# Reordering an attention-plus-S4 kernel, transposing x by DMA, keeping the last inverse matrix resident, and summing the complex product in TensorE

## The chip, the cores and the metric

The kernel runs on one core of one Trainium2 chip. The metric is the device time of one execution, in microseconds (us). One execution of each kernel was also recorded by the hardware profiler; all lines shown below come from such records. The engines are named PE (TensorE, matmuls), PEld (TensorE weight loads), DVE (VectorE), ACT (ScalarE), POOL (GpSimd) and SP (the engine whose queue issues most DMAs). An execution counts as fast unless it is over 1.5% above the fastest of the same kernel; comparisons use fast runs.

Before the change the kernel took 512.9 us (median of three runs, 511.55 to 514.36).

## The reference, cut to what matters

The output is two independent results side by side, both bf16, of 2048 positions by 640 channels.

```python
# part A: 32 heads of 20 channels, each position attends to itself and 7 earlier ones, 2 apart
qkv = x @ wqkv
attn = softmax(where(mask, einsum("bhsd,bhswd->bhsw", q, kg) * Dh**-0.5, -1e9))
o = einsum("bhsw,bhswd->bhsd", attn, vg);  a = o @ wo
# part B: S4 convolution, 640 channels, 192 states each
P = exp(dt * (A_re + 1j*A_im) * l)              # l = 0..2047: the powers
K = einsum("dn,dnl,dn->dl", C, P, dt*B).real    # the convolution kernel
y = irfft(rfft(u, 4096) * rfft(K, 4096))[:2048] + u * Dskip
```

## The kernel before: what the change touches

Part B works in five chunks of 128 channels. For each chunk VectorE builds two tables of powers, X and Y, by complex products of a few base powers; TensorE multiplies them into the convolution kernel `Kd` ("M" below, for make). `Kd` is spread into time order, the FFTs of u and K run as two matmul steps `f1` and `f2`, VectorE multiplies the two spectra, and a first inverse step `ia` gives Z ("F"). A second inverse step turns Z into y for chunks 0 to 2 together and later for 3 and 4 ("I"); y gets u times Dskip ("S"). Part A runs in four blocks: logits and softmax ("L"), weighted values and output projection ("V"). A scheduler interleaves all this at build time; after that every engine runs its instructions in a fixed order.

The base powers of a chunk pair come from ScalarE sines between two VectorE steps, and go through DRAM (`Gd`):

```python
for k in order:                                   # 11 powers of two
    pht = gp.tile(..., name="ph", tag="ph")       # one buffer each
    mct = gp.tile(..., name="mc", tag="mc")
    nc.scalar.activation(out=mc, in_=wi[:, s], func=ACT.Identity, bias=...)
    V.tensor_scalar(out=ph[:, 0], in0=mc, ..., op0=A.logical_shift_left)
    V.tensor_scalar(out=ph[:, 1], in0=wi[:, s], ..., op0=A.logical_shift_left)
    nc.scalar.activation(out=cs..., in_=ph..., func=ACT.Sin, scale=PHS)
    V.tensor_tensor(out=cs, in0=cs, in1=am..., op=A.mult)
    done(k, cs)                                   # DMA of cs to Gd
```

The spectrum product and the first inverse step:

```python
V.tensor_tensor(out=Y,    in0=K, in1=Ur..., op=A.mult)
V.tensor_tensor(out=t[:], in0=K, in1=Ui..., op=A.mult)
V.tensor_tensor(out=Y[:, :, 0], in0=Y[:, :, 0], in1=t[:, :, 1], op=A.subtract)
V.tensor_tensor(out=Y[:, :, 1], in0=Y[:, :, 1], in1=t[:, :, 0], op=A.add)
# ia: 16 j, 2 parts, 4 channel groups: 128 matmuls that each fill a quarter of the output rows
MM(ps[32*g:32*g+32, jj], lhsT=Yf[:, :, r, 4*j+g], rhs=C["EA"][:, r, :], ..., tile_position=(0, 32*g))
```

x comes in eight loads and is transposed by 80 matmuls with the identity, evicted by 24 ScalarE copies. The order of the main program:

```python
gens(..., 0, 1, dst0, done0)       # powers of chunk 0
make(0); a.transpose()
for ct in range(5): a.proj("k", ct)
for ct in range(5): a.proj("q", ct)
batch(1, 3); batch(3, 5)           # powers of chunks 1, 2 and of 3, 4
# ... u is reordered through DRAM ...
for ct in range(5): a.proj("v", ct)
make(1)
for c in range(NCH):
    # F(c), then make(c + 2), then (c < 4) L(c) V(c); for c == 3 the first inverse
inverse([3, 4], ...)
```

The second inverse step loads a quarter of its matrix `HB` at a time (two buffers), in both inverses, so the whole 4 MB comes twice. Each quarter then loads u, multiplies by HB, copies to `ysb` on ScalarE, makes `ud = u * D + ysb` on VectorE (one buffer), and stores.

The softmax here doesn't subtract the row's maximum and nothing guards it: scores larger than these inputs give would overflow.

## Time and profile before

| | before |
|---|---|
| time, median of 3 | 512.9 us |
| profiled execution, span and mean granted clock | 511.0 us, 0.876 |
| first attention product starts | 149.6 us |
| last power table ends | 369.7 us |
| HBM read | 42.86 MB |

The page's busy table, VectorE's row of the 40 slices (each digit the busy tenths of one fortieth of the span), and the chain of work that ended last, in shares of the span:

```profile
PE 368.9 (72%) x5943; PEld 243.2 (48%) x5943; DVE 360.2 (70%) x528; ACT 269.0 (53%) x517; POOL 104.8 (21%) x192
...
DVE  0326899651899997999999977998948753636012
...
PE 36%; DVE 28%; DMA 15%; ACT 12%; issue 6%; SPq 1%; POOL 0%; ACTq 0%; POOLq 0%; DVEq 0%
```

No engine is full over the whole span. VectorE is nearly full in the middle and has gaps at the beginning and the end. Cutting the span at the first attention product and at the end of the last table (within 0.9 us of them) shows the three stages. Columns of the windows view: stretch, its length, busy us (and instructions) of each engine, granted clock, DMA share, GB/s.

```profile
0.00:149.66 149.66, 109.90 (x1015) 56.24 (x1016) 90.10 (x188) 103.12 (x197) 47.88 (x83) 0.94 0.69 186
149.66:368.90 219.24, 166.70 (x3363) 121.96 (x3363) 205.68 (x273) 108.10 (x206) 26.19 (x57) 0.87 0.39 104
368.90:511.00 142.10, 92.25 (x1565) 65.02 (x1564) 64.38 (x71) 57.74 (x115) 30.72 (x52) 0.81 0.51 144
```

The middle stage is VectorE's: 205.68 of 219.24 us. In the first stage the waits view shows VectorE waiting for sines (engine, tile and line waited for, us in total, times, longest):

```profile
DVE cs L212 <- ACT cs L211: 22.3, 10, 9.7
```

In the last stage, loads and stores of the second inverse step stand in the way:

```profile
DVE ud L671 <- DMA out_dram<-ud: 18.3, 4, 8.3
...
PE ps_ib L667 <- DMA zq<-Zdram_61: 8.6, 2, 5.1
...
PE ps_ib L667 <- DMA HB<-k_HB: 8.3, 2, 5.6
```

And two groups that the change replaces, from the page (line, engine, operation, names, shapes and count, then busy us and mean ns of one, then idle before; for the DMA: count, size, us to landing):

```profile
L364 PE MATMUL ps_ia<-cEA,Yf 128*32 128x256 bf16 x640 | 29.1, 333 | 7.9 <-DVE Yf L350 6.7
...
HB<-k_HB SPq DMA_DIRECT2D x8, 1024.0 KB, 6.1
```

### The profile page before, as it was taken

What the parts mean: (1) busy time and instruction counts of PE and PEld (TensorE: products, weight loads), DVE (VectorE), ACT (ScalarE), POOL (GpSimd) and SP (SyncE); (2) the same over time, 40 slices, a digit from 0 to 9 for tenths busy, and PEclk for the clock granted to TensorE, in tenths of its full rate; (3) what the DMA queues carried; (4) which work ended last, traced back from release to release, by engine and by line L of the source; (5) the groups of instructions that cost most, each with busy time, mean ns of one, the idle gap of its engine ahead of it and who ended that gap; (6) DMA issues with size and microseconds to landing.
All of it is one profiled execution on the core that took longest, in us unless ns stands there. A gap on an engine that the chain in (4) does not pass through costs nothing.

```text
span 511.0 us, 13799 instructions
## 1 busy us (share of the span) xinstructions
PE 368.9 (72%) x5943; PEld 243.2 (48%) x5943; DVE 360.2 (70%) x528; ACT 269.0 (53%) x517; POOL 104.8 (21%) x192
## 2 busy tenths in 40 slices
PE   2868799874752778798879868699495855987720
PEld 1543334631220566666656755476263533765520
DVE  0326899651899997999999977998948753636012
ACT  4466895758682435656355723467224522656610
POOL 7605500055000001000170001070001341143012
PEclk9999999997795788799988978999779969997955
DMA  7964946359669352220236432043609597622262
GB/s 197 267 145 129 225 123 208 104 168 255 215 211 314 118 110 66 60 115 3 61 66 204 114 66 57 1 132 83 139 13 347 146 299 192 197 48 39 91 187 41
DMA packets 83596, 70.99 MB, mean 139 GB/s; under 512 B 51744, under 2 KB 75104, under 8 KB 81872
## 3 DMA queue, kind: packets, MB, share of 16 engines
q1 hardware_dynamic: 75456, 55.90, 39.0%
q0 software_dynamic: 6368, 13.16, 10.7%
q10 hardware_dynamic: 1712, 1.07, 0.8%
q8 instruction: 46, 0.75, 0.7%
q14 instruction: 14, 0.11, 0.1%
HBM read 42.86 MB, written 24.13 MB: 131 GB/s over the span
## 4 chain that ended last, share of the span: by engine, by line
PE 36%; DVE 28%; DMA 15%; ACT 12%; issue 6%; SPq 1%; POOL 0%; ACTq 0%; POOLq 0%; DVEq 0%
PE ps_o L493 6%; DVE krtmp L226 4%; PE ps_k L286 4%; PE ps_k L281 4%; PE ps_op L508 3%; DMA Gdram<-cs 3%; DMA xn<-in_A_x_dram 3%; PE ps_s L310 3%; ACT S L344 3%; DMA zq<-Zdram_61 3%; DMA out_dram<-ud 3%; DVE Ytab L225 3%; DVE prod L468 2%; PE ps_p L428 2%; DMA uq<-Udram 2%
## 5 line engine op out<-in xcount | busy, mean ns | idle before, releaser
L468 DVE TENSOR_TENSOR prod<-qb,kb 128x2048 bf16<-128x2048 bf16 x40 | 48.7, 1233 | 2.0 <-PE ps_l L471 2.0
L502 POOL DMA_DIRECT2D oT<-vb x64 | 36.7, 581 | 48.1 <-ACT vb L494 43.8
L429 ACT CAST st<-ps_p 128x512 bf16<-128x512 f32 x60 | 34.1, 581 | 12.6 <-PE ps_p L428 12.3
L428 PE MATMUL ps_p<-xT,w_324 128*128 128x512 bf16 x100 | 28.0, 439 | 13.7 <-ACT st L429 13.6
L364 PE MATMUL ps_ia<-cEA,Yf 128*32 128x256 bf16 x640 | 29.1, 333 | 7.9 <-DVE Yf L350 6.7
L494 ACT CAST vb<-ps_o 128x512 bf16<-128x512 f32 x20 | 13.1, 653 | 37.2 <-PE ps_o L493 37.1
L286 PE MATMUL ps_k<-Ytab,Xtab 64*20 64x33 bf16 x1280 | 25.8, 243 | 9.3 <-issue 9.2
L342 PEld LDWEIGHTS <-cT 128*64 128x64 bf16 x640 | 23.3, 114 | 18.9 <-issue 18.3
L288 ACT CAST Kd<-ps_k 128x363 bf16<-128x363 f32 (+1 forms) x15 | 6.8, 453 | 47.2 <-PE ps_k L286 47.2
L471 PE MATMUL ps_l<-prod,cGs 128*32 128x512 bf16 x160 | 18.3, 435 | 17.6 <-DVE prod L468 17.4
L225 DVE TENSOR_TENSOR Ytab<-Ytab 128x2688 bf16<-128x2688 bf16 (+3 forms) x25 | 30.8, 1234 | 0.0
L364 PEld LDWEIGHTS <-Yf 128*32 128x32 bf16 x640 | 23.3, 174 | 15.3 <-DVE Yf L350 8.2
L226 DVE TENSOR_TENSOR krtmp<-Ytab 128x2688 bf16<-128x2688 bf16 (+3 forms) x25 | 30.4, 1215 | 0.0
L281 PEld LDWEIGHTS <-Xtab 128*20 128x20 bf16 x1280 | 21.9, 125 | 14.9 <-issue 14.2
L493 PEld LDWEIGHTS <-cident 128*128 128x128 bf16 x160 | 14.9, 100 | 28.8 <-issue 14.4
L428 PE MATMUL ps_p<-xT,w_320 128*128 128x512 bf16 x100 | 25.6, 410 | 3.9 <-ACT st L429 2.8
L212 DVE TENSOR_TENSOR cs<-cs,am 128x768 bf16<-128x768 bf16 x22 | 12.2, 556 | 22.3 <-ACT cs L211 22.3
L292 POOL DMA_DIRECT2D Kd<-Kd x20 | 10.1, 514 | 86.6 <-ACT Kd L288 86.2
L286 PEld LDWEIGHTS <-Xtab 64*20 64x20 bf16 x1280 | 21.9, 121 | 12.2 <-issue 10.6
L244 POOL MEMSET Ytab<- 128x192 bf16 x5 | 1.4, 284 | 123.9 <-PE ps_k L286 123.9
L225 DVE TENSOR_TENSOR Xtab<-Xtab,Xg 128x768 bf16<-128x768 bf16 (+2 forms) x35 | 24.7, 706 | 2.2 <-DMA Xg<-Gdram 1.8
L281 PE MATMUL ps_k<-Ytab,Xtab 128*20 128x33 bf16 x1280 | 25.1, 246 | 1.1 <-DVE Ytab L229 0.5
(460 smaller groups left out, 948.7 us busy)
## 6 DMA issues: line engine op xcount, KB each, us to landing
HB<-k_HB SPq DMA_DIRECT2D x8, 1024.0 KB, 6.1
Gdram<-cs SPq DMA_DIRECT2D x24, 192.0 KB, 3.1
kb<-kd SPq DMA_DIRECT2D x4, 710.0 KB, 6.7
vb<-vd SPq DMA_DIRECT2D x4, 710.0 KB, 5.4
xn<-in_A_x_dram SPq DMA_DIRECT2D x8, 320.0 KB, 6.0
us<-in_B_u_dram POOLq DMA_DIRECT2D x16, 160.0 KB, 5.0
Udram<-uc POOLq DMA_DIRECT2D x8, 320.0 KB, 4.0
kd<-st SPq DMA_DIRECT2D x5, 512.0 KB, 5.8
```

Of the source, the lines that this page charges most:

```text
L225: V.tensor_tensor(out=full(O), in0=full(Y), in1=gb(gr), op=A.mult)
L226: V.tensor_tensor(out=full(t), in0=full(Y), in1=gb(gi), op=A.mult)
L281: MM(o, lhsT=X[:, :, part, col], rhs=Y[:, :, part, col], start=False, stop=False, tile_position=(0, 32 * g), skip_group_check=True)
L286: MM(o, lhsT=X[hb:hb + 64, :, part - 2, col], rhs=Y[hb:hb + 64, :, part - 2, col], start=False, stop=(part == 3), tile_position=(hb, 32 * ...
L342: nc.tensor.matmul(ps[64 * dd:64 * dd + 64, kk, r], lhsT=T[:, k, r, :], rhs=A1[:, k, :, 64 * dd:64 * dd + 64], start=(kk == 0 and r == 0), ...
L364: MM(o, lhsT=Yf[:, :, r, 4 * j + g], rhs=C["EA"][:, r, :], start=(jj == 0 and r == 0), stop=(r == 1), skip_group_check=True, tile_position ...
L428: nc.tensor.matmul(ps[:], lhsT=w[:, kt, 128 * ct:128 * ct + 128], rhs=self.xT[:, kt, 512 * sc:512 * sc + 512], start=(kt == 0), stop=(kt = ...
L429: nc.scalar.copy(out=st[:, sc], in_=ps[:])
L468: V.tensor_tensor(out=pr[:], in0=q[:, ct].unsqueeze(1).to_broadcast([128, 4, 4, 128]), in1=windows(k[:, ct, :, 8 - 8 * m:8 - 8 * m + 128], ...
L471: nc.tensor.matmul(ps[32 * sc:32 * sc + 32], lhsT=self.pools["Gs"][:, ct, :], rhs=pr[:, :, sc, :], start=(ct == 0), stop=(ct == 4), tile_p ...
L493: nc.tensor.matmul(ps[:], lhsT=self.ident[:], rhs=p2[:, w], start=(w == 0), stop=(w == W - 1))
L502: nc.gpsimd.dma_start(out=oT[32 * q:32 * q + 32, :, sc, :], in_=self.vb[qb][32 * sc:32 * sc + 32, q:DH:4, HALO:HALO + 128])
```

## The change

The intent has seven parts that are named or easy to see: (1) all base powers are made before the first table; (2) attention blocks move ahead and overlap other work, in an order given by a string; (3) x is transposed by DMA; (4) Z lives in two slots outside the tables' space, so that (5) the inverse matrix can be loaded once and stay; (6) VectorE makes only the four products of the complex multiplication, and TensorE sums them as four accumulated terms with full-width matmuls; (7) u times D is made ahead in four buffers, and the last inverse adds its matmul result to it straight from PSUM.

There are smaller parts that the description does not name: the loads of A, B and C of part B change queues, the phase tiles get a second buffer, the X table gets a new layout and one more product step, 15 zero matmuls go, and the shift of `Kd` moves 7 rows on two queues in place of 12 on one.

The core of the diff (cuts are marked):

```diff
+ORDER = "L0 V0 M1 F0 L1 V1 M2 F1 L2 V2 M3 F2 M4 F3 S012 I012 L3 F4 V3 S34 I34"
# ... constants: EA gets four slots; HB's rows are permuted; X_EXP reordered ...
-        eng[g % 2].dma_start(out=ldt[32 * g:32 * g + 32, :], in_=lsrc[g])
+        nc.scalar.dma_start(out=ldt[32 * g:32 * g + 32, :], in_=lsrc[g])
-            (eng[g % 2] if a < 2 else nc.gpsimd).dma_start(out=nat[a]...)   # eng = [sync, scalar]
+            (nc.gpsimd if a in (2, 3) else nc.sync).dma_start(out=nat[a]...)
# ... powers
-        pht = gp.tile([128, 2, 2 * CW], i32, name="ph", tag="ph")
-        mct = gp.tile([128, 2 * CW], i32, name="mc", tag="mc")
+        pht = gp.tile([128, 2, 2 * CW], i32, name="ph", tag="ph", bufs=2)
+        mct = gp.tile([128, 2 * CW], i32, name="mc", tag="mc", bufs=2)
# ... tables: new layout and steps; kgen: no zero matmul; Kd shift on two queues ...
# ... spectrum product
-        V.tensor_tensor(out=Y, in0=K, in1=Ur..., op=A.mult)
-        V.tensor_tensor(out=t[:], in0=K, in1=Ui..., op=A.mult)
-        V.tensor_tensor(out=Y[:, :, 0], in0=Y[:, :, 0], in1=t[:, :, 1], op=A.subtract)
-        V.tensor_tensor(out=Y[:, :, 1], in0=Y[:, :, 1], in1=t[:, :, 0], op=A.add)
+        for i, u in enumerate((Ur, Ui)):
+            V.tensor_tensor(out=Yf[:, 2 * i:2 * i + 2, :, 32 * b:32 * b + 32], in0=K, in1=u..., op=A.mult)
# ... ia
-            for r in range(2):
-                for g in range(4):
-                    MM(o, lhsT=Yf[:, :, r, 4 * j + g], rhs=C["EA"][:, r, :], ..., tile_position=(0, 32 * g))
+            for q in range(4):
+                nc.tensor.matmul(ps[:, jj]..., lhsT=Yf[:, q, 2 * jq + jj, :], rhs=C["EA"][:, q, :], start=(jj == 0 and q == 0), stop=(q == 3))
# ... x
-        for q in range(8):
-            xn = xw.tile([128, 2, D], bf16, name="xn", tag="xn", bufs=3)
-            nc.sync.dma_start(out=xn[:], in_=xsrc[:, 2 * q:2 * q + 2, :])
+        for q in range(4):
+            nc.sync.dma_start(out=self.xT[:, :, 512 * q:512 * q + 512], in_=self.x[0, 512 * q:512 * q + 512, :], transpose=True)
# ... 80 transposing matmuls and 24 copies go ...
     gens(tc, pools, ta, wi, 0, 1, dst0, done0)
+    batch(1, 3)
+    batch(3, 5)
     make(0)
-    a.transpose()
# ... after the k and q projections
-    batch(1, 3)
-    batch(3, 5)
# ... second inverse step
-            HB = ip.tile([128, 16, 2, 128], bf16, name="HB", tag="HB", bufs=2)
-            nc.sync.dma_start(out=HB[:]..., in_=hsrc[:, s])
+        inv["HB"] = HB = ip.tile([128, 64, 2, 128], bf16, name="HB")   # once, in two DMAs
+    Z = fp.tile([128, 2, 64, 2, 32], bf16, name="Z")
# ... skip(cs): ud = u * D ahead of its inverse, ud with bufs=4 ...
+                if n == 3:
+                    nc.scalar.copy(out=ysb[:, o:o + per], in_=ps[:])
+                else:
+                    V.tensor_tensor(out=ud[:, o:o + per], in0=ps[:], in1=ud[:, o:o + per], op=A.add)
```

In the letters of the order string, the program before ran M1 F0 M2 L0 V0 F1 M3 L1 V1 F2 M4 L2 V2 F3 L3 V3 I012 F4 I34.

## The prediction

> **What bounds the kernel now.** No engine is full: over 511 us TensorE is busy 72%, VectorE 70%, ScalarE 53% (busy table). By windows there are three stages. (1) 0 to 149.7 us, up to the first attention product: VectorE busy 90 us, ScalarE 103, TensorE 110; VectorE waits 22 us in all for sines (waits view). (2) 149.7 to 368.9, up to the end of the last power table: VectorE 206 of 219 us, so VectorE-bound. (3) 368.9 to 511, 142 us: TensorE 92, VectorE 64, ScalarE 58. The chain of waits shows loads of skip input (8.4 us), Z (9.6, 4.8), inverse matrix (5.6, 2.7), stores (7.2, 3.8), and the last chunk's FFT running alone.
>
> **What the change does, with durations from the trace.**
> - VectorE: the 40 add/subtracts of the complex product go (17.2 us). X tables get one more step, about +0.7 us per chunk. 360 becomes about 346 us.
> - ScalarE: 24 transposed-x copies (12.0 us) and 8 of the last inverse (4.7) go: 269 to about 252.
> - TensorE: 80 transposes (11 us) and 15 zero matmuls (5.9) go. The inverse-A step has 64 full 128x256 matmuls per chunk instead of 128 quarter ones: 36 ns each (56 in 2.01 us) becomes about 105 (the 128x256 spread matmuls run at 100), so +2 us per chunk. Net 369 to about 360.
> - DMA: the inverse matrix is loaded once, not twice (4 MB less), ahead of its use. x comes by four DMA transposes; no trace shows one. The Trainium skill (DMA: Bandwidth & Descriptors, "Latency and other measured facts") states 261 GB/s; my estimate from it is 10 us for 2.6 MB.
> - Order: all powers come before the first table; chunk 1's table now precedes the first product; attention block 3 overlaps the first inverse; only chunk 4's FFT and the short inverse follow.
>
> **On the critical path.** Summing durations along VectorE's new order: about 132 us precede the first product (89 before), about 167 lie between it and the last table (207 before), 44 follow. ScalarE has about 108 us up to the end of the powers and phase tiles are double-buffered, so VectorE starves less: the first product stays near 152 us with 43 us more VectorE work done. The middle shrinks to about 190 us (TensorE also has about 187 there), so the last table ends near 342 instead of 369. Tail: table-to-kernel matmuls 10, rest of chunk 3's FFT 20, first inverse with attention products 21, chunk 4's FFT 32 (ScalarE-bound: 44 evictions of about 0.65 us), output projection and last inverse 17, stores 5 to 8: about 107 instead of 142, because most waits for Z, matrix and skip input go.
>
> **Predicted: 455 us**, 8 in 10 between 432 and 482. Faster by over 2%: 0.93; within 2%: 0.05; slower: 0.02.
>
> **What would show it.** First product at 145 to 165 us; VectorE over 85% busy before it. Last table at 330 to 355. From there about 107 us to the end, with under 8 us of TensorE waiting for matrix or Z. VectorE busy about 346, TensorE 360, ScalarE 252. Inverse-A matmuls about 105 ns apart. DMA transposes landing before 30 us.
>
> **What would make it wrong.** DMA transposes much slower than 261 GB/s: ScalarE's fixed order has projection copies between sines, so a late x stalls the powers and everything after (+10 to +25 us). The powers' trip through DRAM delaying chunk 1's table. The inverse matrix reuses the table's space, so its load starts only after the last table matmuls; landing late, it holds the first inverse. [...]

## The result, and the profile after

The changed kernel took 466.03 us (median of four runs, 464.76 to 469.33) against 512.23 us for the kernel before (four runs). The ratio is 0.911, with a 95% interval of 0.904 to 0.918. Every ratio in this document is the mean time of one kernel's fast runs over that of the kernel before in the same rounds, so it is not quite the ratio of the medians quoted. The output was correct.

| | before | predicted | after |
|---|---|---|---|
| time | 512.2 us | 455 (432 to 482) | 466.0 us |
| first attention product starts | 149.6 | 152 (145 to 165) | 146.1 |
| last power table ends | 369.7 | 342 (330 to 355) | 354.7 |
| from there to the end | 141 | 107 | 108 |
| busy TensorE / VectorE / ScalarE | 369 / 360 / 269 | 360 / 346 / 252 | 367 / 347 / 254 |
| HBM read | 42.86 MB | | 36.18 MB |

The row of HBM reads overstates what was saved. Of what went, 4.19 MB are the second load of the inverse matrix (with it back, u_hb below reads 40.37 MB), but 2.62 MB are x itself: with the plain loads back, u_xpose reads 38.80 MB although its DMAs move the same 66.7 MB in all. So in these runs the count leaves out what the DMA transposes read. (The longer `EA` adds 0.13 MB.)

The page of the changed kernel, as shown of before:

```profile
PE 367.2 (79%) x5528; PEld 241.2 (52%) x5528; DVE 347.0 (75%) x513; ACT 254.0 (55%) x485; POOL 97.1 (21%) x173
...
DVE  1599797999599974899979899999998074740413
...
PE 38%; DVE 35%; DMA 9%; ACT 8%; issue 7%; POOL 1%; SPq 1%; POOLq 0%; DVEq 0%; ACTq 0%
...
L351 PE MATMUL ps_ia<-cEA,Yf 128*128 128x256 bf16 x320 | 37.7, 276 | 3.6 <-DVE Yf L341 3.6
...
HB<-k_HB SPq DMA_DIRECT2D x2, 2048.0 KB, 7.9
```

DMA has fallen from 15% to 9% of the chain that ended last and ScalarE from 12% to 8%; the two engines that do the arithmetic now hold 73% of it. The first inverse step costs TensorE 8.6 us more over five chunks (37.7 against 29.1). The windows, cut at the same two events:

```profile
0.00:146.20 146.20, 95.98 (x894) 45.05 (x895) 116.59 (x238) 91.06 (x168) 44.38 (x72) 0.84 0.74 193
146.20:354.30 208.10, 188.13 (x3184) 132.67 (x3185) 189.60 (x232) 108.55 (x209) 32.24 (x67) 0.93 0.45 117
354.30:463.00 108.70, 83.08 (x1467) 63.47 (x1457) 40.81 (x46) 54.44 (x109) 20.51 (x34) 0.89 0.47 130
```

In the middle stage TensorE and VectorE are now both near 90% busy. VectorE did 26.5 us more before the first product (116.59 against 90.10), not the 43 us of the prediction.

The waits view of the first stage, and TensorE's longest waits of the last stage:

```profile
PE ps_p L400 <- ACT st L401: 30.8, 6, 14.2
...
ACT cs L214 <- DMA Gdram<-cs: 12.5, 9, 3.1
...
DVE cs L215 <- ACT cs L214: 8.0, 7, 3.0
```

```profile
PE ps_o L465 <- DVE p_7379 L462: 3.1, 1, 3.1
...
PE ps_ia L351 <- DVE Yf L341: 1.8, 1, 1.8
```

The waits for Z and for the inverse matrix are gone from the last stage, as predicted. VectorE's wait for sines fell from 22.3 to 8.0 us. New are ScalarE's wait for stores of the powers, 12.5 us, and a longer wait of the projections for their ScalarE copies, 30.8 us (17.6 before).

The DMA queue of the SP engine in the first 33 us (start us, us, and the issues of one kind together):

```profile
10.95 1.78 SPq L129 DMA_DIRECT2D nat_88<-in_B_B_im_dram  x4
12.77 19.98 SPq L379 DMA_TRANSPOSE xT<-in_A_x_dram  x4
```

Four transposes of 640 KB keep the issuing queue for 20 us. That is 131 GB/s (2.62 MB over 20 us), half of what the prediction took from the Trainium skill. Other loads ran beside them: from 12.77 to 32.75 us all DMAs together moved 238 GB/s (windows view), so 131 GB/s is what x got in company, not the rate of a transpose alone.

### The profile page after: what moved, and what is told of

The parts are those of the page before. It is cut to its first block, busy times and chain, and to the rows that moved or that the text cites. A ratio compares the mean times of both kernels' runs of the same rounds, so it can differ in the third digit from the quotient of the medians.

```text
span 463.0 us, 12916 instructions
## 1 busy us (share of the span) xinstructions
PE 367.2 (79%) x5528; PEld 241.2 (52%) x5528; DVE 347.0 (75%) x513; ACT 254.0 (55%) x485; POOL 97.1 (21%) x173
## 3 DMA queue, kind: packets, MB, share of 16 engines
HBM read 36.18 MB, written 24.13 MB: 130 GB/s over the span
## 4 chain that ended last, share of the span: by engine, by line
PE 38%; DVE 35%; DMA 9%; ACT 8%; issue 7%; POOL 1%; SPq 1%; POOLq 0%; DVEq 0%; ACTq 0%
PE ps_o L465 9%; PE ps_k L280 7%; DVE krtmp L223 7%; PE ps_ia L351 5%; DMA Gdram<-cs 4%; DVE prod L440 4%; DVE Ytab L223 3%; DVE Yf L341 3%; ACT S L338 3%; PE ps_s L304 3%; DVE Xtab L223 2%; DVE Ytab L225 2%; PE ps_op L480 2%; DVE Ytab L224 2%; PE ps_l L443 2%
## 5 line engine op out<-in xcount | busy, mean ns | idle before, releaser
L280 PE MATMUL ps_k<-Ytab,Xtab 128*20 128x33 bf16 (+1 forms) x2560 | 52.8, 245 | 6.9 <-issue 6.0
L280 PEld LDWEIGHTS <-Xtab 128*20 128x20 bf16 (+1 forms) x2560 | 45.3, 126 | 19.4 <-issue 15.5
L400 PE MATMUL ps_p<-xT,w_309 128*128 128x512 bf16 x100 | 34.3, 512 | 25.1 <-ACT st L401 21.5
L341 DVE TENSOR_TENSOR Yf<-S 128x1024 bf16<-128x1024 bf16 x40 | 25.6, 683 | 27.6 <-ACT S L338 27.6
L351 PE MATMUL ps_ia<-cEA,Yf 128*128 128x256 bf16 x320 | 37.7, 276 | 3.6 <-DVE Yf L341 3.6
L353 ACT CAST Z<-ps_ia 128x512 bf16<-128x512 f32 x40 | 23.5, 586 | 25.6 <-PE ps_ia L351 25.2
L400 PEld LDWEIGHTS <-w_309 128*128 128x128 bf16 x100 | 11.9, 122 | 47.1 <-issue 38.8
L351 PEld LDWEIGHTS <-Yf 128*128 128x128 bf16 x320 | 31.1, 99 | 10.0 <-DVE Yf L341 5.6
L443 PE MATMUL ps_l<-prod,cGs 128*32 128x512 bf16 x160 | 22.3, 431 | 9.5 <-DVE prod L440 9.3
L223 DVE TENSOR_TENSOR krtmp<-Xtab,Xg 128x768 bf16<-128x768 bf16 (+2 forms) x40 | 26.0, 651 | 0.5
L214 ACT ACTIVATE cs<-ph 128x768 bf16<-128x768 int32 x22 | 17.9, 846 | 12.5 <-DMA Gdram<-cs 12.5
L480 PE MATMUL ps_op<-wo,oT 128*128 128x320 bf16 x160 | 23.0, 299 | 2.0 <-ACT ob L481 2.0
```

The lines of the kernel that those rows point to most:

```text
L223: V.tensor_tensor(out=o[0], in0=Y[0], in1=gr, op=A.mult)
L280: MM(ps[32 * g:32 * g + 20, i, :], lhsT=X[rows, part % 2, :, col + t0 + i], rhs=Y[rows, :, part % 2, col + t0 + i], start=(part == 0 and i ...
L341: V.tensor_tensor(out=Yf[:, 2 * i:2 * i + 2, :, 32 * b:32 * b + 32], in0=K, in1=u.unsqueeze(1).to_broadcast([128, 2, 16, 32]), op=A.mult)
L351: nc.tensor.matmul(ps[:, jj].rearrange("p l r d -> p (l r d)"), lhsT=Yf[:, q, 2 * jq + jj, :], rhs=C["EA"][:, q, :], start=(jj == 0 and q ...
L353: nc.scalar.copy(out=Z[:, :, :, 4 * jq:4 * jq + 4].rearrange("p l r (j d) -> p (l r) j d", d=2), in_=ps[:].rearrange("p j l r d -> p (l r) ...
L400: nc.tensor.matmul(ps[:], lhsT=w[:, kt, 128 * ct:128 * ct + 128], rhs=self.xT[:, kt, 512 * sc:512 * sc + 512], start=(kt == 0), stop=(kt = ...
```

## The experiments

Twelve runs followed, in the order of the table. The first four are set against the 0.911 of the result, so differences there carry the uncertainty of both intervals. "M", "F", "L" and so on are the letters explained above.

| label | what it is | median us | ratio to before (95%) |
|---|---|---|---|
| (result) | the change | 466.03 | 0.911 (0.904 to 0.918) |
| u_order | change, old order of blocks | 466.64 | 0.915 (0.909 to 0.922) |
| u_four | change, old product and first inverse | 475.36 | 0.934 (0.928 to 0.940) |
| u_hb | change, inverse matrix in quarters | 474.58 | 0.932 (0.928 to 0.937) |
| u_xpose | change, x transposed by TensorE | 480.60 | 0.943 (0.937 to 0.950) |
| after_ref | the change again | 467.23 | 0.910 (0.900 to 0.919) |
| u_ob | change, old order and powers late | 460.10 | 0.901 (0.894 to 0.908) |
| cs4 | change, four buffers for powers | 468.44 | 0.917 (0.910 to 0.924) |
| v_f4first | change, chunk 4's FFT earlier | 472.30 | 0.923 (0.916 to 0.930) |
| after_5 | the change, five rounds | 465.65 | 0.913 (0.910 to 0.917) |
| u_ob_5 | as u_ob, five rounds | 459.07 | 0.899 (0.895 to 0.903) |
| u_batch_5 | change, powers late only | 464.48 | 0.903 (0.897 to 0.909) |
| b_three | before, with three parts of the change | 507.01 | 0.994 (0.989 to 0.999) |

All outputs were correct. The first theory (A in most of the texts) was the prediction's own account of where the gain comes from; B is the rival named there.

### u_order: the old order of blocks

```diff
-ORDER = "L0 V0 M1 F0 L1 V1 M2 F1 L2 V2 M3 F2 M4 F3 S012 I012 L3 F4 V3 S34 I34"
+ORDER = "M1 F0 M2 L0 V0 F1 M3 L1 V1 F2 M4 L2 V2 F3 L3 V3 S012 I012 F4 S34 I34"
```

> The changed kernel with the old order of blocks (attention block after the next chunk's table, first inverse after all attention, fourth... fifth chunk's FFT after it); all else as changed. Theory A (the gain of the last stage, 142 to 109 us, comes mainly from the new order, which lets attention block 3 and the first inverse share the time): 482 to 492 us, ratio to the kernel before 0.94 to 0.96. Rival B (the last stage gained because waits for the inverse matrix and Z went and work was removed; order hardly matters): within 5 us of the changed kernel's 466, ratio 0.905 to 0.92.

It took 466.64 us, ratio 0.915, the same as the change. Its windows, cut at the same two events:

```profile
0.00:150.10 150.10, 96.83 (x908) 46.07 (x909) 120.67 (x245) 93.13 (x170) 42.35 (x72) 0.86 0.74 191
150.10:324.90 174.80, 152.78 (x2923) 113.03 (x2925) 154.93 (x203) 92.72 (x176) 23.14 (x51) 0.89 0.38 105
324.90:464.70 139.80, 113.84 (x1715) 81.53 (x1703) 72.79 (x69) 68.80 (x140) 29.68 (x50) 0.92 0.54 141
```

The last table ends at 324.9 us instead of 354.7, and the stage after it takes 139.8 us instead of 108.7, nearly as long as before the change. The end is the same. So the tail that shrank by 33 us is where the table was put, not time saved: the old order leaves two attention blocks after the last table, the new one leaves one, and the tail's busy times say so (TensorE 113.84 against 83.08 us, VectorE 72.79 against 40.81). Theory A fell.

### u_four: the old complex product and first inverse step

The subtract and add of the complex product and the 128 quarter matmuls come back (with the constants and layouts that go with them).

> The changed kernel with the complex product as before (two products, one subtract, one add on VectorE, and 128 quarter matmuls per chunk in inverse A). VectorE gains 17.2 us of work, TensorE loses 2 to 3 us per chunk. Theory A (VectorE is what bounds the middle stage, so removing its work pays nearly in full): +11 to +16 us, 477 to 482, ratio 0.932 to 0.942. Rival B (TensorE is as full as VectorE there, so the trade is nearly even): -2 to +5 us, 464 to 471, ratio 0.905 to 0.92.

It took 475.36 us, ratio 0.934. Against the change's 0.911 that is 0.023 of 509 us, or 11.6 us. VectorE's busy time in its profile is 367.9 us in place of 347.0, so 20.9 us of VectorE work cost 11.6 us of time. This part of the change pays: the size lies at the lower end of theory A's range and clear of B's, but it is little more than half of the removed work, not "nearly in full".

### u_hb: the inverse matrix streamed in quarters

```diff
-        inv["HB"] = HB = ip.tile([128, 64, 2, 128], bf16, name="HB")
-        # ... loaded once, in two DMAs
+            HB = ip.tile([128, 16, 2, 128], bf16, name="HB", tag="HB", bufs=2)
+            nc.sync.dma_start(out=HB[:]..., in_=hsrc[:, s])      # in each quarter of both inverses
```

> The changed kernel with the inverse matrix streamed in quarters, twice, through two buffers as before. Theory A (only the last inverse waits for it, 8 us in the trace of before, and the first inverse now has attention to hide behind): +4 to +9 us, 470 to 475, ratio 0.918 to 0.928. Rival B (the resident matrix is a main part of the gain): +12 us or more, ratio over 0.935.

It took 474.58 us, ratio 0.932: 10.8 us more than the change. TensorE's waits of the whole run show where:

```profile
PE ps_ib L675 <- DMA HB<-k_HB: 11.5, 2, 6.8
```

Both waits lie in the last inverse, where TensorE has nothing else left to run. From its first matmul to the end of the span this inverse takes 25.1 us here (446.7 to 471.8) and 14.9 us in the changed kernel (448.0 to 463.0), which is 10.2 of the 10.8 us. The measured size lies between what the two theories gave; the resident matrix is worth about 11 us in this kernel.

### u_xpose: x transposed by TensorE again

The eight loads, 80 matmuls and 24 ScalarE copies come back, ahead of the projections. The tile `xn` has two buffers here and three in the kernel before, because with three the kernel does not fit the memory that the change leaves. The missing buffer shows little: TensorE waits 5.1 us for loads of x here and 5.5 us in the kernel before.

> The changed kernel with x transposed by TensorE and copied by ScalarE as before (x loaded through two buffers, not three, for space). ScalarE gains 12 us and TensorE 11 us of work, all before 40 us. Theory A (ScalarE feeds VectorE with sines in the first stage, so its 12 us are on the path): +6 to +12 us, ratio 0.922 to 0.935. Rival B (the first stage is bound by VectorE and by the powers' trips through DRAM; transposes fit in slack): -2 to +3 us, ratio 0.905 to 0.917.

It took 480.60 us, ratio 0.943: 16.4 us more than the change, more than theory A's 6 to 12. TensorE's longest wait:

```profile
PE ps_xt L400 <- ACT xT L402: 33.0, 13, 15.4
```

The transposing matmuls wait 33 us for their ScalarE copies, which stand behind exponentials and sines in ScalarE's fixed order. During the longest wait (15.4 us, up to 52.4 us) ScalarE even sits idle for 2.74 us, with two finished transposes to copy, because the entry ahead of the copies waits for VectorE:

```profile
51.51 0.62 ACT L211 ACTIVATE mc<-wi,quarter 128x384 int32<-128x384 int32 x1 [2.74 <-DVE ph L212]
52.03 0.84 ACT L402 CAST xT<-ps_xt 128x256 bf16<-128x256 f32 x2
```

The Trainium skill ("TensorE: Matmul & The Clock Gate", section "Architectural detail: the array is 16× 32×32, not 1× 128×128") says that ScalarE and VectorE are strict FIFO; these lines agree. With powers first, ScalarE's queue is full of sines just when x arrives. So 16.4 us is what the DMA transposes are worth given the new place of the powers; in the old place it need not be that much.

### u_ob and u_ob_5: both reorderings undone

```diff
-ORDER = "L0 V0 M1 F0 ... S34 I34"
+ORDER = "M1 F0 M2 L0 V0 ... F4 S34 I34"       # as in u_order
-    batch(1, 3)                # ahead of make(0)
-    batch(3, 5)
     make(0)
     # ... k and q projections ...
+    batch(1, 3)
+    batch(3, 5)
```

> The changed kernel with the old order of blocks and with the powers of chunks 1 to 4 made after the key and query projections as before: both parts of the change that only reorder are undone, all removed work and waits stay removed. Theory A (the order matters only through what the engines can do while they would starve; with powers late VectorE starves again in the first stage): +6 to +14 us against the reference, ratio 0.925 to 0.94. Rival B (as with the order of blocks alone, the total is set by the work and by the waits removed, not by the order): within 4 us of the reference, ratio 0.905 to 0.92.

> Again the changed kernel with both reorderings undone, in more rounds. If undoing them is neutral: ratio 0.906 to 0.916, as the reference. If the reorderings really cost time: 0.897 to 0.905, below the reference with intervals apart.

It took 460.10 us the first time (0.901) and 459.07 us in five rounds (0.899, 0.895 to 0.903), where the change in the same rounds took 465.65 us (0.913, 0.910 to 0.917). The intervals lie apart: the two reorderings together cost about 7 us (0.0141 of 510 us). Neither theory had this: A expected a loss of 6 to 14 us from undoing them, B no more than 4 us either way. This kernel is faster than both the kernel before and the changed one. Its windows:

```profile
0.00:132.00 132.00, 95.13 (x916) 46.56 (x926) 96.07 (x217) 91.14 (x172) 45.34 (x72) 0.96 0.82 217
132.00:321.70 189.70, 158.53 (x2971) 118.84 (x2980) 178.64 (x233) 97.89 (x187) 23.07 (x51) 0.90 0.38 103
321.70:456.70 135.00, 105.09 (x1620) 75.42 (x1623) 69.14 (x65) 63.16 (x127) 29.59 (x50) 0.91 0.53 137
```

VectorE does 96 us of work before the first product, only 6 us more than before the change, and still the first product starts 17.6 us earlier than before. The prediction had the opposite: that powers first is what makes room.

### u_batch_5: only the powers back in their late place

> The changed kernel with only the powers put back after the key and query projections, the new order of blocks kept. If powers first is what delays the first attention product (146 us, against 132 with both reorderings undone) and costs time: first product near 132 us and ratio 0.897 to 0.906. If the two reorderings only pay or cost together: within 0.005 of the reference, or above it.

The six runs spread from 454.97 to 466.72 us. Four of them are classed slow because they lie over 1.5% above the fastest, so the ratio of 0.903 (0.897 to 0.909) rests on two runs. Its profiled run, one of the fast ones, had its first product at 127.4 us. The median of all six, 464.48 us, lies just below the change's. It points the same way as u_ob, that the early powers cost time, but with this spread the run does not tell how the 7 us divide between the powers and the blocks. A better pointer is u_order against u_ob: with the old order of blocks in both, the powers' place alone makes 0.915 against 0.901, though on two chips.

### cs4: four buffers for the powers on their way to DRAM

```diff
-            cst = gp.tile([128, 2, 2, CW], bf16, name="cs", tag="cs", bufs=2)
+            cst = gp.tile([128, 2, 2, CW], bf16, name="cs", tag="cs", bufs=4)
```

> The changed kernel with four buffers, not two, for the powers on their way to DRAM. In the changed kernel ScalarE waits 12.5 us in all (9 times) for stores of powers to free a buffer, 1.3 us in the kernel before. Theory A (these waits delay sines and so VectorE in the first stage): -3 to -8 us against the reference, first attention product before 142 us. Rival B (VectorE has table work to do meanwhile): within 2 us of the reference, the first product moves by less than 2 us.

It took 468.44 us, ratio 0.917: no gain. ScalarE's wait for the stores of the powers falls from 12.5 us to 4.0, and the last power's sine comes 17 us sooner (93.7 us instead of 110.5); the first product starts at 148.2 us all the same (146.1 in the result's profile, 144.3 in after_ref's). A wait that is new and visible was not one that mattered.

### v_f4first: chunk 4's FFT ahead of the first inverse

```diff
-... F3 S012 I012 L3 F4 V3 S34 I34"
+... F3 F4 L3 V3 S012 I012 S34 I34"
```

> The changed kernel with chunk 4's FFT moved ahead of attention block 3 and of the first inverse, so that the stretch in which ScalarE alone sets the pace (413 to 444 us in the trace of the changed kernel) can share the time with attention. Theory A (the tail is a chain with free engines beside it, so overlap pays): -5 to -12 us against the reference, ratio 0.885 to 0.90. Rival B (order hardly matters, as the run with the old order of blocks suggests): within 3 us of the reference.

It took 472.30 us, ratio 0.923, about 6 us slower than the change (465.7 us is the mean of after_ref's fast runs, 471.8 the mean here); the two intervals overlap a little (0.916 to 0.930 and 0.900 to 0.919). The idea was that the last chunk's FFT, which ran nearly alone for 31 us (413 to 444 us), should be covered by other work. Theory A fell: there is no gain, and the order in the change is probably the better one of the two.

### after_ref and after_5: the change again

> The changed kernel unchanged, for a reference on this chip and in these rounds: ratio to the kernel before 0.904 to 0.918.

> The changed kernel unchanged, as the reference of these rounds: ratio to the kernel before 0.905 to 0.916.

Both repeat the result: 467.23 us (0.910) with one slow run of four, and 465.65 us (0.913).

### b_three: three parts of the change alone, in the kernel before

The kernel before gets the DMA transposes, the four-term sum, and the resident matrix with Z in two slots (U has one buffer, as in the change; otherwise it does not fit). Order of blocks, place of powers, queues of the input loads, single phase buffers, tables, and the second inverse's sums stay as they were.

> The other way round: the kernel before with only three parts of the change (DMA transposes of x; four-term sum without adds; resident inverse matrix, with Z in two slots and one buffer for u, without which it finds no space), in the old order, with the old table layout, old zero matmuls and old inverse otherwise. If these three parts are nearly the whole gain (undone one at a time they cost 11.6, 10.8 and 16.4 us, 39 in all): ratio 0.90 to 0.93, 460 to 475 us. If each needs the reordering to pay: over 0.94.

It took 507.01 us, ratio 0.994 (0.989 to 0.999). The theory that these three are nearly the whole gain fell. The rival, that they need the reordering to pay, does not fit either: u_ob_5 has the old order too and is the faster for it. The page's busy table shows how much work went without a gain:

```profile
PE 361.2 (71%) x5519; PEld 240.5 (47%) x5543; DVE 342.8 (67%) x488; ACT 258.7 (51%) x493; POOL 104.5 (21%) x192
```

VectorE has 17 us less to do than before, TensorE 8 and ScalarE 10, close to the prediction's list of removed work, and the kernel is 3 us faster. u_ob_5, with the same order of blocks and the same place of the powers, has about the same busy times (343.9, 358.8 and 252.2 us) and takes 48 us less. Its windows:

```profile
0.00:162.60 162.60, 94.84 (x925) 46.74 (x936) 94.58 (x199) 91.67 (x170) 47.92 (x83) 0.91 0.73 183
162.60:355.70 193.10, 153.41 (x2898) 113.82 (x2905) 178.47 (x228) 94.69 (x177) 25.99 (x57) 0.84 0.33 91
355.70:508.90 153.20, 112.97 (x1698) 79.96 (x1702) 69.75 (x64) 72.36 (x146) 30.62 (x52) 0.92 0.49 128
```

Against u_ob_5 the first stage is 30.6 us longer and the last 18.2 us; the middle is nearly equal. VectorE's busy time is the same within 2 us in every stage, so the difference is waiting. Against the kernel before, the first stage is 13 us longer, the middle 26 us shorter and the last 11 us longer, so the 3 us are a gain and losses together. In the first stage these are VectorE's two waits that u_ob_5 does not have at this size (3.1 and 2.4 us there):

```profile
DVE pr L176 <- PE ps_tr L148: 26.1, 1, 26.1
...
DVE Xtab L227 <- DMA Xg<-Gdram: 11.0, 1, 11.0
```

VectorE waits from 14.9 to 40.9 us for the matmuls that turn B (6.4 us for the same ones in the kernel before). The DMA queue and TensorE say why:

```profile
5.18 27.45 SPq L387 DMA_TRANSPOSE xT<-in_A_x_dram  x4
```

```profile
22.03 2.29 PE L408 MATMUL ps_p<-xT,w 128*128 128x512 bf16 x5 [10.81 <-DMA xT<-in_A_x_dram]
27.06 1.01 PE L408 MATMUL ps_p<-xT,w 128*128 128x512 bf16 x2 [2.74 <-DMA xT<-in_A_x_dram]
27.87 0.31 PE L148 MATMUL ps_tr<-cident,nat 128*128 128x64 bf16 x2
...
39.81 0.32 PE L148 MATMUL ps_tr<-dg,nat 128*128 128x64 bf16 x2
```

In b_three the loads of B and C are on another queue, the transposes are issued at 5.2 us, and the scheduler placed projections (`ps_p`) ahead of the matmuls that turn C and B (`ps_tr`). TensorE keeps that order, sits for 10.8 us until the first quarter of x lands, and reaches B at 39.8 us. In the changed kernel and in u_ob_5 the loads of B stand ahead of the transposes on the same queue, the transposes start at 12.8 and 13.2 us, and the scheduler placed all the turns of A, C and B ahead of the first projection: TensorE starts B at 20.2 and 20.6 us.

In the last stage, the time from the last inverse's first matmul to the end is 23.7 us (485.2 to 508.9) in b_three and 13.5 us (443.2 to 456.7) in u_ob_5. In b_three VectorE waits there 11.1 us for the stores that hold its single `ud` buffer, as it did before the change (18.3 us). The other 8 of the 18.2 us are not traced here.

## Why the prediction was right or wrong

**The time and the direction were right.** 466 us lies in the range, 11 us above the estimate. That it does is in part luck: one named reason for the gain, powers first (tested together with the new order of blocks), costs about 7 us, and the three parts that carry most of the counted work gain only 3 us without the rest of the change (both below).

**Right, with numbers.** First product at 146 us (predicted 145 to 165); tail 108 (107); last table at 354.7 (330 to 355, at the very edge); VectorE busy 347 (346); ScalarE 254 (252). No waits for Z or the matrix in the tail. TensorE was 367 (360) in this run. The same kernel showed 366.1 us in after_ref's profile and 360.5 in after_5's, at granted clocks of 0.889, 0.890 and 0.918, so the miss is no larger than what differs between profiles of one kernel.

**The term that was mis-sized: VectorE's work in the first two stages.** The text says: "about 132 us precede the first product (89 before), about 167 lie between it and the last table (207 before)", and from it "43 us more VectorE work done" and "The middle shrinks to about 190 us". Measured: 116.6 us before the first product, 189.6 in the middle, and a middle of 208 us. The 132 is a sum of durations; the 89 beside it is a busy time. VectorE's instructions overlap each other in the trace, so the two must not be subtracted. Counted alike from the traces, the durations of the instructions that start before the first product add to 102.8 us before the change and 132.9 us after it, which is 30 us more and not 43. After the change the 238 instructions before the first product have durations that add to 132.9 us, while VectorE was busy 116.59 us. A piece of the trace shows it (start us, us):

```profile
144.44 0.56 DVE L223 TENSOR_TENSOR Xtab<-Xtab,Xg 128x768 bf16<-128x768 bf16 x1
144.92 0.55 DVE L223 TENSOR_TENSOR krtmp<-Xtab,Xg 128x768 bf16<-128x768 bf16 x1
145.39 0.55 DVE L223 TENSOR_TENSOR Xtab<-Xtab,Xg 128x768 bf16<-128x768 bf16 x1
```

Instructions of 0.55 us start 0.47 us apart. The work that had seemed done early was left for the middle stage: 189.6 in place of 167 is 22.6 us more, and that stage came out 18 us longer than said. Of the 22.6 us, 16.5 are the difference between the 43 and the measured 26.5; the other 6 stay open. (The prediction's 132, 167 and 44 add to 343 us, close to the busy total, while all durations in the changed kernel add to 379 us. So only the first of the three is a sum of durations; how the 167 was worked out is not on record.) The first stage came out 6 us shorter and the tail 2 us longer. The predicted stages add to 449 us and the measured ones to 463, which is these 14 us; the estimate of 455 stood 6 us above its stages and the time stands 3 us above the span, which leaves the miss of 11. The Trainium skill ("Perfetto Trace Analysis", section "Optimizing Scalar/DVE Operations") says that profiled latency of these engines is about twice the engine-busy overhead, "since the write-acknowledgement half overlaps with the next instruction"; the 80 ns here agree in kind. It was there to be read before the prediction and was not used.

**The share of time before the first product** was predicted over 85% for VectorE; it was 80% (116.6 of 146.2), for the same reason.

**The DMA transposes** were said to take 10 us, "my estimate from it", and to land before 30 us. They took 20 us of the issuing queue, and TensorE's last wait for x ended at 32.5 us. The Trainium skill ("DMA: Bandwidth & Descriptors", section "Latency and other measured facts") gives 261 GB/s for a DMA transpose, from one kernel; here x came at 131 GB/s while all DMAs together moved 238 GB/s. The estimate left out the loads beside it; what a transpose reaches alone, no run here shows. In the changed kernel TensorE waited only 3.6 us for x: 120 matmuls of part B were placed ahead of the first projection, 40 in b_three. In b_three the same transposes cost 14.5 us of waits. The prediction's warning ("DMA transposes much slower than 261 GB/s") named the right danger and the wrong victim: it was VectorE, behind TensorE's fixed order.

**First inverse matmuls** were to be "about 105 ns apart". In the trace 64 of them take 7.9 and 7.2 us in the last two chunks, where no other work comes between, 123 and 113 ns each; four quarter matmuls took four times 36, or 144 ns, before. The prediction's "run at 100" looks like a mean over two shapes: in the trace of the kernel before, 128x256 spread matmuls start 109 ns apart and 128x128 ones 56. The skill ("TensorE: Matmul & The Clock Gate", section "Part 3: Packing small matmuls — row/col tiling") says that small matmuls at different tile positions run concurrently in the array; the 36 ns of a quarter matmul agree, against 113 to 123 ns of a full-width one over the same 256 columns. So the change does twice the products at 8.6 us more TensorE time in all.

**Where the account of the gain failed.** The prediction said that the time falls because VectorE's work is less, because powers first let it start more of it early, and because most waits of the tail go. The second was tested and fell, and the third holds only in part. Powers first and the new block order are not needed: undoing both gains 7 us more (u_ob_5). The tail's 33 us are the place of a mark: with the old order the tail is 139.8 us and the total the same (u_order). What is real in it is the last inverse, which took 29.4 us from its first matmul to the end before and takes 14.9 us now. The sum of removed work is not what was gained either: b_three removes 17, 8 and 10 us of the three engines and gains 3.

**Where the gain came from, as far as the runs show it.** From above, taking one part back out of the change costs 11.6 us (four-term sum), 10.8 (resident matrix) and 16.4 (DMA transposes), which add to 39 us. From below, putting the same three into the kernel before gains 3 us. Both are measured. The parts are not independent: a wait that another wait hides gives nothing when it is removed alone (in cs4, 8.5 us of a wait went and nothing was gained). The last inverse shows the other side: 29.4 us before, 25.1 in u_hb (four `ud` buffers, streamed matrix), 23.7 in b_three (resident matrix, one `ud` buffer), 14.9 with both, so each alone gives about 5 us and the two together 14.5. What lies between b_three and u_ob_5, 48 us, is the parts whose gain in time the prediction did not estimate one by one, although it named the phase buffers and counted the busy time of some others: input loads queued ahead of the transposes, second phase buffers, the new table layout without zero matmuls, `Kd`'s shift on two queues, and the skip products ahead with four buffers and a sum straight from PSUM. The trace says that in the first stage most of the 30.6 us is VectorE waiting behind TensorE for the turns of B (26.1 us against 3.1), and that some 10 us at the end is the single `ud` buffer and the extra copy. These are readings of traces: no run changed the queue of the loads alone, or the skip buffers alone, so how the 48 us divide is open.

## What to carry to other kernels

Do not set a sum of durations beside a busy time: take the busy time of a window for both, or correct the sum by the start-to-start distance. A stage that gets shorter is no gain until the same run's end moves, so test an explanation by stages with a kernel whose mark sits elsewhere. When a slow load moves onto a queue, see what each engine's fixed order puts behind its first user: here the same three improvements were worth 3 us with part B's loads on another queue and the projections in front, and belonged to a gain of about 50 us with everything else of the change in place. That the queue and the order make most of that difference in the first stage is read from the traces; no run changed them alone.

## What the Trainium skill lacked or had wrong

- "DMA: Bandwidth & Descriptors", section "Latency and other measured facts": 261 GB/s for a DMA transpose "with non-contiguous mid-dim", "~350-400 GB/s" in the contiguous case. It does not say what a transpose gets beside other loads. Here four transposes of 640 KB (bf16, 512 rows of 640 each) took 20.0 us of the issuing queue in the changed kernel and 27.5 us in b_three, 131 and 96 GB/s, while all DMAs together moved 238 and 210 GB/s; so the figures are not refuted, but an estimate from them was half the time.
- The same page, section "Issuing engines are not separate DMA queues", says that the issuing time "is usually small relative to the DMA itself". For these transposes it was not: the queue was held 3.1 to 6.8 us each in the changed kernel and up to 8.6 in b_three (there a median of 7.8 us, with 11.8 us from issue to landing), and nothing else was issued on it for 20 and 27 us. The page gives no issue time of a transpose that is said to be measured on trn2.
- "Perfetto Trace Analysis", section "Optimizing Scalar/DVE Operations", has the overlap of successive VectorE instructions, in a parenthesis. It does not say what follows for reading a trace: 238 instructions with durations of 132.9 us were 116.6 us of busy time, about 69 ns of overlap each.
- No page that was read says how to weigh a scheduler's fixed order on TensorE: in b_three, with one late input in front of them (10.8 us of waiting for x), matmuls that do not use it stood 19 us later than in u_ob_5 (39.8 against 20.6 us), and VectorE waited 26.1 us for them.
